# Twelve token runs a batch of 508 and 504 columns in place of ten of 512 and two of 480

## The chip, the cores and the metric

The kernel runs on one core of one Trainium2 chip. The metric is the device time of one execution in microseconds (us). The core has a matrix engine (TensorE, PE in the profile; PEld is its weight load), a vector engine (VectorE, DVE), a scalar engine (ScalarE, ACT), GpSimd (POOL, unused here but for four constants) and a sync engine (SyncE, SP) that issues transfers. Matmul results land in PSUM, which has eight banks of 512 fp32 columns; everything else lies in SBUF.

## What is computed

A gated scan over the tokens of two sequences of 6080 tokens with 256 channels, and then a feed-forward block with 2048 hidden units on all 12160 tokens.

```
f = lower_bound + (1 - lower_bound) * sigmoid(f_logit)
i = 1 - f
for t in range(S):
    h = f[:, t] * h + i[:, t] * x[:, t]
    y[:, t] = h
hid = y.reshape(B * S, D) @ w_in             # 256 -> 2048
g = hid * clip(hid + 3, 0, 6) / 6
out = g @ w_out                              # 2048 -> 256
```

## The kernel before

Everything is kept transposed: channels lie on the 128 partitions, tokens along the columns. The tokens of each of the two sequences are cut into twelve runs, and `token_runs` (L185) lists them in order of position, the two sequences in turn, as (sequence, first token, number of tokens n). With 6080 tokens it makes ten runs of 512 and two of 480 a sequence, 24 runs in all, numbered h = 0 to 23. The n of a run is the number of columns of every matmul, of every ScalarE and VectorE instruction and of every transfer of this run; no other size in the program hangs on it, and all tiles are allocated 512 columns wide whatever n is.

A run goes through these stages:
- `scan_x` (L344) loads f_logit and x, forms the gate on ScalarE and VectorE and runs the scan along the tokens (L387). The last state of a run starts the scan of the next one of the sequence. For h = 0 the work is cut into two halves of n/2 columns.
- `split` (L400) makes two fp32r tensors of each fp32 tensor, the rounded value (hi) and the remainder (lo). A product is then three fp32r matmuls: hi by hi, hi by lo, lo by hi.
- The first product and the gate. The first four runs (`DIRECT`, L109) are `direct` (L569): 16 blocks of 128 hidden units with 6 matmuls each. The other 20 runs go in pairs, one run of each sequence at the same position, through `quad` (L655): a scheme of seven products in place of eight for a block of two by two, 8 quads of 7 products of 3 matmuls a pair (matmuls in `product`, L620). Sums that the scheme needs are taken on ScalarE and VectorE (L599, L609, L611).
- The second product, `mm2` (L499, matmuls in L512), adds up over the hidden blocks in a PSUM bank: 2 halves of 3 matmuls for each block. From the second pair on, the first four blocks (`GROUP`, L21) of the second product go through the seven-product scheme too (`chain`, L738).
- `evict` (L540) scales by 1/6 and stores.

Counted out, the four direct runs have 192 products of 128 x 128 weights each (a few of them are done in fp32 from the unsplit weights, L509 and L585), the first pair has 360 fp32r matmuls and each of the nine later pairs has 354. At the start, fillers on zeros (L836) keep TensorE busy between the first matmuls.

The order on every engine is fixed before the run. Each piece of work is a `Job` with a modelled cost that depends on n (`act_cost`, `dve_cost`, `pe_cost`, L87 to L96); `ordered` (L117) walks through the jobs by due times and gives the order in which each engine's instructions are issued, and this is repeated five times with the starts found. The matmuls of a pair are interleaved with the second product of the pair before it by a fixed table (`FILLS`, L22).

Of the kernel before, what the change touches and what calls it, by code (L numbers as in the profile page):

```python
# [18 lines left out]
BANK = 512  # L19
# [165 lines left out]
def token_runs(B, S):  # L185


    runs = []
    full = (S - 1) // BANK - 1
    rest = S - full * BANK  # L190
    counts = [BANK] * full + [-(-rest // 2), rest // 2]
    assert counts[-1] == counts[-2] <= BANK
    s = 0
    for n in counts:
        runs.extend((b, s, n) for b in range(B))
        s += n
    return runs
# [3 lines left out]
def gated_scan_then_ffn(  # L201
# [10 lines left out]
    NF = w.shape[1]  # L212
    KD = D // P
    runs = token_runs(B, S)
    assert B == 2 and KD == 2 and NF % 4 == 0 and len(runs) > 4 and len(runs) % 2 == 0
    pairs = [(h, h + 1) for h in range(DIRECT, len(runs), 2)]
# [652 lines left out]
```

## Time and profile before

| what | us |
|---|---|
| median of 3 runs (lowest, highest) | 1001.44 (1000.84, 1001.79) |
| the profiled execution, as timed | 1001.43 |
| its span, first to last instruction | 999.6 |
| TensorE busy in it | 988.1 (99%) |
| VectorE busy | 854.0 (85%) |
| ScalarE busy | 691.5 (69%) |

The profiled execution takes 1.83 us more than its span. In the rows further down, an engine's line gives its busy time and its number of instructions. A matmul's recorded time runs until its last result and overlaps the next matmul, so the distance between the starts of two matmuls is shorter than the time of one. The chain of work that ended last is followed back from the last instruction: each piece is work that released the next one or that ran just before it on the same engine, and successive pieces of one line are merged, with their number.

### The profile page before, as it was taken

The numbers are of one execution on the slowest core, as the hardware profiler recorded it, in microseconds if no ns is written. First come the engines' busy times: TensorE is split into PE (matmuls) and PEld (weight loads), VectorE is DVE, ScalarE is ACT, GpSimd is POOL, SyncE is SP. The second block draws the span as 40 slices with busy tenths as digits, with TensorE's granted clock in tenths as the row PEclk, the third lists the DMA queues.
The fourth block names the chain that finished last, engine by engine and source line by source line (L and its number), as shares of the span: only waits on it lengthen the run. The fifth ranks groups of instructions, "written<-read, shape, count | busy, mean of one in ns | idle before, by whom it ended". The sixth has DMA issues, their size and how long they took to land.

```text
span 999.6 us, 11737 instructions
## 1 busy us (share of the span) xinstructions
PE 988.1 (99%) x4343; PEld 811.2 (81%) x4343; DVE 854.0 (85%) x1131; ACT 691.5 (69%) x1101; POOL 0.2 (0%) x4
## 2 busy tenths in 40 slices
PE   9999999999899999999999999999999999999998
PEld 3778888888688888888888888888888888888887
DVE  7997658998999989988988998998998898898863
ACT  7975656666768659668667766866875866866752
POOL 0000000000000000000000000000000000000000
PEclk9999999999999999999999999999999999999999
DMA  9751030010002002003003001100200200300101
GB/s 360 269 168 45 22 106 22 0 64 22 22 32 95 1 22 106 1 3 125 1 0 127 1 1 59 68 0 32 95 1 22 101 1 1 122 0 1 41 1 40
DMA packets 25898, 54.89 MB, mean 55 GB/s; under 512 B 2288, under 2 KB 6896, under 8 KB 25840
## 3 DMA queue, kind: packets, MB, share of 16 engines
q1 hardware_dynamic: 25424, 53.87, 15.1%
q8 instruction: 34, 0.56, 0.2%
q10 hardware_dynamic: 416, 0.26, 0.1%
q14 instruction: 24, 0.20, 0.1%
HBM read 41.67 MB, written 12.45 MB: 54 GB/s over the span
## 4 chain that ended last, share of the span: by engine, by line
PE 94%; DVE 3%; issue 1%; ACT 1%; DMA 0%; SPq 0%; ACTq 0%
PE bank L620 46%; PE bank L512 40%; PE bank L575 8%; PE bank L585 1%; DVE xt L387 1%; DMA wst<-w 0%; DVE xt L377 0%; DVE r L483 0%; PE bank L509 0%; DVE xlo L415 0%; DVE xt L246 0%; ACT ft L365 0%; DVE wst L290 0%; DVE glo L565 0%; ACT xhi L408 0%
## 5 line engine op out<-in xcount | busy, mean ns | idle before, releaser
L481 ACT ACTIVATE r<-bank 128x512 f32<-128x512 f32 (+1 forms) x304 | 179.7, 592 | 136.9 <-PE bank L620 105.9
L483 DVE SCALAR_TENSOR_TENSOR r<-r,bank 128x512 f32<-128x512 f32 (+1 forms) x304 | 205.5, 677 | 47.5 <-ACT r L481 46.4
L512 PE MATMUL bank<-ghi,whi 128*128 128x512 f32 (+1 forms) x620 | 240.5, 388 | 0.0
L512 PE MATMUL bank<-glo,whi 128*128 128x512 f32 (+1 forms) x620 | 240.2, 387 | 0.0
L512 PE MATMUL bank<-ghi,wlo 128*128 128x512 f32 (+1 forms) x620 | 240.2, 387 | 0.0
L620 PE MATMUL bank<-xhi,wst 128*128 128x512 f32 (+1 forms) x640 | 234.6, 387 | 1.7 <-DVE bank L611 1.7
L620 PEld LDWEIGHTS bank<-xhi,wst 128*128 128x128 f32 x640 | 120.1, 188 | 26.0 <-DVE bank L611 2.1
L412 DVE SCALAR_TENSOR_TENSOR glo<-r,ghi 128x1024 fp32r<-128x1024 f32 (+1 forms) x98 | 118.2, 1206 | 23.7 <-ACT ghi L406 23.6
L512 PEld LDWEIGHTS bank<-ghi,wlo 128*128 128x128 f32 x620 | 116.3, 188 | 23.4 <-DVE wlo L294 0.2
L512 PEld LDWEIGHTS bank<-ghi,whi 128*128 128x128 f32 x620 | 116.3, 188 | 23.3 <-issue 0.2
L512 PEld LDWEIGHTS bank<-glo,whi 128*128 128x128 f32 x620 | 116.3, 188 | 23.3
L620 PE MATMUL bank<-xlo,wst 128*128 128x512 f32 (+1 forms) x320 | 123.8, 387 | 0.0
L406 ACT ACTIVATE ghi<-r 128x1024 fp32r<-128x1024 f32 (+1 forms) x98 | 102.6, 1047 | 17.7 <-PE bank L512 9.8
L415 DVE TENSOR_TENSOR glo<-r,ghi 128x1024 fp32r<-128x1024 f32 (+1 forms) x89 | 106.6, 1204 | 3.9 <-ACT ghi L408 3.8
L408 ACT CAST ghi<-r 128x1024 fp32r<-128x1024 f32 (+1 forms) x89 | 92.2, 1037 | 15.2 <-PE bank L512 12.5
L611 DVE TENSOR_TENSOR bank<-bank,e 128x512 f32<-128x512 f32 (+1 forms) x80 | 55.3, 691 | 28.0 <-PE bank L620 20.3
L620 PEld LDWEIGHTS bank<-xlo,wst 128*128 128x128 f32 x320 | 60.0, 188 | 11.9
L481 ACT ACTIVATE r<-e 128x512 f32<-128x512 f32 (+1 forms) x80 | 49.7, 621 | 26.1 <-DVE e L609 26.1
L620 PE MATMUL bank<-xhi,whi 128*128 128x512 f32 (+1 forms) x160 | 62.0, 387 | 1.0 <-ACT bank L599 1.0
L620 PE MATMUL bank<-xlo,whi 128*128 128x512 f32 (+1 forms) x160 | 61.9, 387 | 0.0
L620 PE MATMUL bank<-xhi,wlo 128*128 128x512 f32 (+1 forms) x160 | 61.9, 387 | 0.0
L599 ACT ACTIVATE bank<-bank 128x512 f32<-128x512 f32 (+1 forms) x80 | 46.1, 576 | 22.7 <-PE bank L620 22.3
(95 smaller groups left out, 1369.3 us busy)
## 6 DMA issues: line engine op xcount, KB each, us to landing
outT<-o SPq DMA_DIRECT2D x40, 256.0 KB, 2.0
ft<-fT SPq DMA_DIRECT2D x19, 512.0 KB, 5.1
xt<-xT SPq DMA_DIRECT2D x18, 512.0 KB, 6.0
wst<-w SPq DMA_DIRECT2D x14, 512.0 KB, 4.3
wst<-w SPq DMA_DIRECT2D x14, 511.5 KB, 5.7
ft<-fT SPq DMA_DIRECT2D x4, 480.0 KB, 4.5
xt<-xT SPq DMA_DIRECT2D x4, 480.0 KB, 5.2
outT<-o SPq DMA_DIRECT2D x4, 240.0 KB, 2.0
```

The costliest lines, as they stand in the source:

```text
L387: nc.vector.tensor_tensor_scan(xt.get()[:, k, o:e], ft.get()[:, k, o:e], xt.get()[:, k, o:e], init, op0=ALU.mult, op1=ALU.add if negative ...
L406: nc.scalar.mul(to(hi), cut(src), -1.0)
L408: nc.scalar.copy(to(hi), cut(src))
L412: nc.vector.scalar_tensor_tensor(out=to(lo), in0=cut(src), scalar=-1.0, in1=to(hi).bitcast(F32), op0=ALU.mult, op1=ALU.subtract)
L415: nc.vector.tensor_tensor(to(lo), cut(src), to(hi).bitcast(F32), op=ALU.subtract)
L481: b = job("ACT", act_cost(n, psum=True), lambda: nc.scalar.activation(r.get()[:, i, :n], src.get()[:, :n], AF.Relu, bias=3.0, scale=-1.0 i ...
L483: return job("DVE", dve_cost(n), lambda: nc.vector.scalar_tensor_tensor(out=r.get()[:, i, :n], in0=r.get()[:, i, :n], scalar=6.0, in1=src. ...
L512: nc.tensor.matmul(bank.get()[:, :n], wt[f][:, D + m * P:D + (m + 1) * P], g.get()[:, half, :n], start=(start and i == 0), stop=(stop and ...
L575: nc.tensor.matmul(ph.get()[:, o:e], wt[f][:, k * P:(k + 1) * P], x[h].get()[:, k, o:e], start=(i == 0), stop=(i == len(ops) - 1),)
L599: nc.scalar.mul(out.get()[:, :n], src.get()[:, :n], -1.0)
L611: nc.vector.tensor_tensor(o, x, y, op=ALU.add)
L620: nc.tensor.matmul(bank.get()[:, :n], wt(), x(), start=(start and z == 0 and i == 0), stop=(z == len(parts) - 1 and i == 2), skip_group_ch ...
```

## The change

`token_runs` makes twelve runs a sequence of nearly equal length, in multiples of 4: eight of 508 tokens and then four of 504. Nothing else is edited. The number of runs, pairs, matmuls, other instructions and transfers stays. The direct runs (positions 0 and 1), the first pair (position 2) and the pairs at positions 3 to 7 have 508 columns, those at 8 to 11 have 504. The halves of h = 0 have 254 columns. The first token of a run is now a multiple of 508 up to 4064, and 504 further on from there.

```diff
     runs = []
-    full = (S - 1) // BANK - 1
-    rest = S - full * BANK
-    counts = [BANK] * full + [-(-rest // 2), rest // 2]
-    assert counts[-1] == counts[-2] <= BANK
+    count = -(-S // BANK)
+    base = S // count // 4 * 4
+    longer, rest = divmod(S - count * base, 4)
+    assert not rest and base + 4 * (longer > 0) <= BANK
     s = 0
-    for n in counts:
+    for i in range(count):
+        n = base + 4 * (i < longer)
         runs.extend((b, s, n) for b in range(B))
         s += n
     return runs
```

## Rows read from the trace of the kernel before

**Rows 1.** Busy time and share by engine; chain by engine; span and granted clock
```profile
PE 988.1 (99%) x4343; PEld 811.2 (81%) x4343; DVE 854.0 (85%) x1131; ACT 691.5 (69%) x1101; POOL 0.2 (0%) x4
...
PE 94%; DVE 3%; issue 1%; ACT 1%; DMA 0%; SPq 0%; ACTq 0%
...
core 0: 999.6 us, clock 1.000
```
**Rows 2.** Stretches: length, busy us and instructions by engine, clock, DMA share, GB/s
```profile
0.00:60.00 60.00, 56.81 (x209) 35.82 (x209) 52.10 (x84) 48.70 (x92) 0.20 (x4) 1.00 0.77 280
60.00:200.00 140.00, 139.73 (x616) 115.70 (x617) 106.21 (x163) 86.92 (x149) 0.00 (x0) 1.00 0.16 57
...
264.00:275.00 11.00, 6.49 (x26) 4.41 (x25) 10.93 (x17) 8.10 (x13) 0.00 (x0) 1.00 0.00 0
275.00:825.00 550.00, 550.00 (x2428) 455.40 (x2428) 493.00 (x608) 394.25 (x607) 0.00 (x0) 1.00 0.11 41
...
860.00:999.60 139.60, 136.06 (x628) 117.31 (x627) 105.70 (x139) 85.73 (x135) 0.00 (x0) 1.00 0.08 27
```
**Rows 3.** TensorE's groups, shapes kept apart: count, busy us, mean ns
```profile
L512 PE MATMUL bank<-ghi,whi 128*128 128x512 f32 x524 | 204.3, 390 | 0.0
...
L575 PE MATMUL bank<-xhi,whi 128*128 128x512 f32 x116 | 36.6, 397 | 1.5 <-DVE r L483 1.5
L512 PE MATMUL bank<-ghi,whi 128*128 128x480 f32 x96 | 36.3, 378 | 0.0
...
L620 PEld LDWEIGHTS bank<-xhi,wst 128*128 128x128 f32 x640 | 120.1, 188 | 26.0 <-DVE bank L611 2.1
```
**Rows 4.** The chain in order of time: start us, us, what, matmuls
```profile
31.59 1.39 PE bank L575 x6
...
597.09 1.36 PE bank L512 x6
...
615.45 17.68 PE bank L620 x78
...
837.54 1.39 PE bank L512 x6
...
855.66 16.90 PE bank L620 x78
```
**Rows 5.** TensorE in order of time after a stall and with 480 columns
```profile
273.45 0.39 PE L620 MATMUL bank<-xlo,wst 128*128 128x512 f32 x1
...
274.61 0.39 PE L512 MATMUL bank<-ghi,whi 128*128 128x512 f32 x1
...
899.91 0.38 PE L512 MATMUL bank<-ghi,wlo 128*128 128x480 f32 x1
900.13 0.37 PE L512 MATMUL bank<-glo,whi 128*128 128x480 f32 x1
900.34 0.38 PE L512 MATMUL bank<-ghi,whi 128*128 128x480 f32 x1
```
**Rows 6.** TensorE in order of time: the matmuls that it waited for
```profile
60.27 0.73 PE L575 MATMUL bank<-xhi,whi 128*128 128x512 f32 x2 [1.45 <-DVE r L483]
...
266.44 0.50 PE L620 MATMUL bank<-bhi,whi 128*128 128x512 f32 x1 [1.85 <-DVE e L609]
...
269.08 0.50 PE L620 MATMUL bank<-xhi,whi 128*128 128x512 f32 x1 [0.99 <-ACT bank L599]
...
273.12 0.50 PE L620 MATMUL bank<-xhi,wst 128*128 128x512 f32 x1 [1.68 <-DVE bank L611]
```
**Rows 7.** VectorE in order of time: the same line at two widths
```profile
249.51 1.22 DVE L415 TENSOR_TENSOR glo<-r,ghi 128x1024 fp32r<-128x1024 f32 x1
...
986.50 1.16 DVE L415 TENSOR_TENSOR glo<-r,ghi 128x960 fp32r<-128x960 f32 x1 [1.43 <-ACT ghi L408]
```
**Rows 8.** In order of time: the last matmul and the last eviction
```profile
995.68 0.38 PE L512 MATMUL bank<-glo,whi 128*128 128x480 f32 x1
...
996.10 0.66 DVE L548 TENSOR_SCALAR r<-bank 128x480 f32<-128x480 f32 x1 [3.24 <-PE bank L512]
```

## What the change should do to the time

> **What bounds the kernel now.** I began with the engines' shares and the chain of work that ended last. TensorE is busy for 988.1 of 999.6 us and holds 94% of the chain; the granted clock is 1.000, its level of 2.4 GHz, throughout [rows 1]. The table by stretches says where this is not so: TensorE falls short in the first 60 us, in 264 to 275 us (VectorE 10.93 of 11 us busy) and at the very end. From 275 to 825 us it is never idle, and after that only behind the last matmul [rows 2, 8]. The stalls are the 1.45 us at 60.27 and the three at 266.44, 269.08 and 273.12 of together 4.52 us [rows 6]. So the time is set by the interval from the start of one matmul to the start of the next, and only that can move it by much. A matmul's recorded duration (389 or 378 ns) overlaps its neighbours' and is not the interval.
>
> The intervals come from the chain, whose merged pieces cover a stated number of matmuls without a gap. With 512 columns 78 of them take 17.68 us: 226.67 ns each. With 480, 78 take 16.90 us: 216.67 ns each [rows 4]. At 2.4 GHz a column takes 0.4167 ns, so 512 columns stream in 213.33 ns and 480 in 200.00 ns. What is left beyond streaming is 13.33 ns at 512 and 16.67 ns at 480: the shorter one is dearer by 3.33 ns than the fixed rest would make it. That is the gap on which the change can gain.
>
> The same rows hold a second thing. The interval at 512 is not one number. Six 512-column matmuls at 837.54, right behind matmuls with 480, take 1.39 us, where six normally take 1.36; six early ones among fp32 matmuls take 1.39 too [rows 4]. That is 231.67 ns, 18.33 ns beyond streaming. After the stall at 273.12, the five intervals from 273.45 to 274.61 take 1.16 us, 232 ns each, and from then on the intervals are even again [rows 5]. So 226.67 is a value that 512 settles into after being disturbed, not a plain sum of streaming and a constant. With 480 the settled intervals alternate: the starts from 899.91 on are 0.22 and 0.21 us apart in turn, and two together take 0.43 us, 433.33 ns by the long row [rows 4, 5]. As an estimate from these sums: 226.67 is 34 times 6.667 ns, and 433.33 is 65 times 6.667 ns. Both settled patterns are whole multiples of 6.667 ns, which is 16 columns at 2.4 GHz.
>
> **The change, part by part.** Matmuls. By the groups of matmuls with their shapes kept apart [rows 3], fp32r matmuls with 512 columns are 3 x 524 (second product), 3 x 116 (direct first product) and 1344 + 3 x 98 (L620, in eleven more groups of the same view), together 3558; those with 480 are 3 x 96, 336 and 3 x 28, together 708. The rest of the 4343 are 36 fp32 records and 41 fillers. Run by run these are 720 in the four direct runs, 360 in the first pair and 354 in each of nine later pairs. The change keeps the number, 4266. It gives 508 columns to the direct runs, the first pair and five later pairs (720 + 360 + 5 x 354 = 2850 matmuls) and 504 to four pairs (1416). The columns streamed are 2,161,536 before and 2,161,464 after, so nothing is gained or lost there (0.03 us). Before, the intervals sum to 3558 x 226.67 + 708 x 216.67 = 806.5 + 153.4 = 959.9 us.
>
> No row shows 504 or 508 columns, so their interval is bounded from both sides by the nearest rows. Lower end: 512's settled 13.33 ns beyond streaming holds at any width, that is 225.00 and 223.33 ns; sum 641.2 + 316.2 = 957.5 us, 2.4 us less. Upper end: they never settle and pay 512's unsettled 18.33 ns, that is 230.00 and 228.33 ns; sum 978.8 us, 18.9 us more. Between them: the 480's 16.67 ns gives 228.33 and 226.67 ns, 971.7 us, 11.8 us more. And if a settled interval must be a multiple of 6.667 ns: 33 of them, 220.00 ns, would leave 8.3 or 10.0 ns beyond streaming, less than the 13.33 ns that are the least of any long row, so 34 remain, 226.67 ns for both widths. Then all 4266 take 226.67 ns: 967.0 us, 7.1 us more.
>
> I take the last value. The nearest row is 512's: 508 and 504 lie 4 and 8 columns from it and 28 and 24 from 480. A settled interval is what long rows show, and 225.00 ns can't keep its place in a pattern of 6.667 ns, while 226.67 can. In this reading the columns taken away from the 512s return nothing, and the last 708 matmuls lose the 10.0 ns that their 480 columns had saved: 708 x 10.0 ns = 7.1 us.
>
> The Trainium skill, page "TensorE: Matmul & The Clock Gate", section "Back-to-back issue gap", gives N / 2.4 + 2.5 ns for back-to-back matmuls; by that rule columns and count alone decide, and the change would be worth 0.03 us. The trace disagrees on the constant: the rule gives 215.8 ns for 512 and 202.5 for 480, where the chain shows 226.67 and 216.67 [rows 4].
>
> Weight loads. Their number and shape stay; each takes 188 ns in the groups at every width [rows 3], under the shortest interval, so they add nothing unless 480's interval is a floor that they set, and 504 and 508 lie above that floor.
>
> fp32 matmuls. 36 records lose 4 or 2 columns in two passes: 0.1 us less, before 30 us, where the weights' arrival decides anyway. Taken at 0.
>
> VectorE and ScalarE. Instruction counts stay and columns too. A view of the first n columns of two halves is one run of 1024 now and two runs of 508 later; the 960-column form is already two runs and takes 1.16 us against 1.22 us for 1024 [rows 7], 0.06 us for 64 columns, so the break costs nothing. VectorE is 493 of 550 us busy in the settled stretch [rows 2], 90%, and stays there; in the last pairs it rises from 76% with 504 for 480 columns and stays covered by TensorE. In 264 to 275 us it is the bound; its 10.93 us shrink by at most 4/512, 0.1 us. The order that the planner writes may come out otherwise there: between all 4.52 us saved and as much lost; the row itself says 4.52, and I take no change.
>
> DMA. Loads and stores keep their count; 512 KB become 508 or 504, 480 KB become 504. Rows now start at multiples of 2032 bytes instead of 2048. From 60 us on the queues are busy 0 to 16% [rows 2] and loads are issued ahead, which is the cover; in the first 60 us (77%) four direct runs move 0.8% less. Taken at 0, within 0.2 us.
>
> The end. The last matmul starts at 995.68, the last eviction of 480 columns takes 0.66 us and the span ends at 999.6 [rows 8]. 24 more columns add 0.03 us there by VectorE's 0.06 us for 64 columns, and some hundredths in the transfer: 0.1 us, which meets the 0.1 us saved above.
>
> Sum, against the profiled execution (1001.43 us, 1.83 us above its span, the same as the median of 1001.44): 1001.4 + 7.1 = 1008.5 us.
>
> **The rivals.** Faster: the 13.33 ns hold at any width, and 216.67 ns is a floor that only widths under 488 meet. Place: the last two pairs, 708 x 3.33 ns; the time is 1001.4 - 2.4, and 0.2 us of it goes into the stalls at 60 and 264 us, which don't end earlier because TensorE comes sooner: 999.2 us. It decides if a 508-column matmul takes 225.4 ns or less. For it: 226.67 and 216.67 fit a fixed rest with a floor. Against it: the 231.67 ns rows, which say that the rest is not fixed.
>
> Much slower: 504 and 508 never settle. 971.7 to 978.8 us of intervals, less some tenths hidden in the stalls: 1013 to 1020 us. For it: every stretch that is not settled 512 leaves 16.67 ns or more beyond streaming. Against it: 480 has a settled pattern of its own.
>
> No change: the interval is a straight line through both points, 225.42 and 224.17 ns, sum 959.9 us: 1001.4 us. Only two points speak for it. The rule of the Trainium skill cited above would give this time too.
>
> Half way: 508 keeps 226.67 ns and 504 alternates 33 and 34 times 6.667 ns (223.33 ns): 2.4 us more, 1003.8 us. Or a multiple of 33 for both after all: 21.4 us less; nothing shows so small a rest.
>
> **How the numbers follow.** All short widths at 226.67 ns: 0.36, 1008.5 us. Never settled: 0.25. Fixed rest with floor: 0.18. Straight line: 0.09. Half way: 0.07. 33 multiples: 0.05. The range reaches from the floor's case, 998.8, to the unsettled bound, 1020; that leaves out the last case and the ends of the others. A difference under 0.2% (2.0 us) is about what a measurement of this kernel can't tell from none. Faster than 999.4 takes 0.12 of the floor's 0.18 and the 0.05, and 0.02 for a kinder order at 264 us: 0.19. Within 2.0 us: 0.06 of the floor, 0.08 of the line and 0.01 of the half way: 0.15. Slower: 0.66.
>
> **What would show it.** The chain's merged pieces: 78 matmuls of 508 at 17.68 us and 78 of 504 at 17.68 us bear the forecast; 17.55 and 17.42 us bear the floor; 17.8 us or more the unsettled case. The starts after a stall should be back at even steps within a dozen matmuls. TensorE should stay idle only where it is now; an added stall after 275 us, or the three at 264 us changed by over 1 us, would make the time wrong for another reason than the interval.

## The result and the profile after

The changed kernel takes 1015.15 us (median of 4 runs, 1014.11 to 1015.56); the kernel before took 1001.62 us beside it. The ratio is 1.0134, with a 95% interval of 1.0117 to 1.0152: 13.5 us slower. The forecast was slower by 7.1 us, 1008.5, with a range to 1020. So the sign and the main mechanism came out, and 6.4 us were not in the sum. The profiled execution of the changed kernel took 1014.11 us with a span of 1012.3; against the 1001.43 and 999.6 of before that is 12.7 us, and it is this difference that is taken apart here.

The page of the changed kernel, busy time and instructions by engine, answers to [rows 1]:

```profile
PE 999.6 (99%) x4345; PEld 814.3 (80%) x4346; DVE 855.5 (85%) x1130; ACT 692.8 (68%) x1102; POOL 0.2 (0%) x4
```

So does its span with the mean granted clock:

```profile
core 0: 1012.3 us, clock 0.996
```

Three things differ that the prediction had as unchanged. VectorE has one instruction less (1131 before) and ScalarE one more (1101 before); TensorE has two matmuls more (4343 before), both of them fillers on zeros in the first 60 us, of which there are 43 in place of 41; and the mean clock is 0.996 where it was 1.000. The first is small to look at and turns out to be worth 3 us.

The chain in order of time (start us, us, what, matmuls), as in [rows 4]. The first piece has 508 columns, the others 504:

```profile
540.19 17.75 PE bank L621 x78
...
701.35 17.68 PE bank L621 x78
...
861.83 17.68 PE bank L621 x78
```

With 504, 78 matmuls take the forecast 17.68 us, 226.67 ns each, exactly what 512 took before. With 508 they take 17.75 us, 227.6 ns each: slower than both 504 and 512. (The mean over some 2700 settled intervals with 508 is 227.62 ns.)

The matmuls for which TensorE waited, as in [rows 6]; the number in brackets is the idle time before:

```profile
61.47 0.74 PE L576 MATMUL bank<-xhi,whi 128*128 128x508 f32 x2 [2.87 <-DVE r L484]
...
271.39 0.79 PE L621 MATMUL bank<-xhi,whi 128*128 128x508 f32 x1 [2.52 <-ACT bank L600]
...
277.02 0.50 PE L621 MATMUL bank<-xhi,wst 128*128 128x508 f32 x1 [1.26 <-DVE bank L612]
```

And the table by stretches behind these stalls and in the settled part (length, busy us and instructions by engine, clock, DMA share, GB/s), as in [rows 2]:

```profile
61.40:67.00 5.60, 5.53 (x17) 4.45 (x18) 4.15 (x8) 3.56 (x7) 0.00 (x0) 0.70 0.63 205
271.30:274.60 3.30, 3.21 (x8) 2.62 (x9) 2.90 (x6) 2.61 (x5) 0.00 (x0) 0.54 0.00 0
...
278.00:825.00 547.00, 547.00 (x2407) 451.66 (x2406) 486.23 (x602) 389.13 (x603) 0.00 (x0) 1.00 0.12 41
```

The stall at 60 us has doubled, from 1.45 to 2.87 us, and the granted clock behind it is a mix of its two levels, 0.70 over 5.6 us, where the kernel before had 1.00:

```profile
61.40:67.00 5.60, 5.60 (x26) 4.60 (x25) 5.24 (x10) 4.10 (x7) 0.00 (x0) 1.00 0.82 252
```

At 264 to 278 us the stalls are shorter (2.52 and 1.26 us in place of the three of together 4.52), but there too the clock falls. In the settled part TensorE is never idle, as before.

With the same matmul set beside the same matmul in both traces, the 12.7 us divide like this. Up to 43 us the changed kernel is 0.3 us ahead. From there to 70 us, around the stall, it loses 3.1 us. Then 0.95 ns with each 508-column matmul, about 2.7 us by 700 us. At 264 to 278 us, 0.2 us net. Where 504 stands in place of 512 (700 to 830 us) next to nothing (0.1 us). Where 504 stands in place of 480, 10.0 ns with each of the last 708 matmuls, 7.0 us. The experiments ask three things: what rule gives these intervals, whether the 3.1 us belong to the widths at all, and whether a better choice of widths exists.

### The profile page after: what moved, and what is told of

It reads as the page before. It is cut to its first block, busy times and chain, and to the rows that moved or that the text cites. A ratio compares the mean times of both kernels' runs of the same rounds, so it can differ in the third digit from the quotient of the medians.

```text
span 1012.3 us, 11760 instructions
## 1 busy us (share of the span) xinstructions
PE 999.6 (99%) x4345; PEld 814.3 (80%) x4346; DVE 855.5 (85%) x1130; ACT 692.8 (68%) x1102; POOL 0.2 (0%) x4
## 4 chain that ended last, share of the span: by engine, by line
PE 95%; DVE 2%; ACT 1%; DMA 1%; issue 0%; ACTq 0%; SPq 0%; DVEq 0%
PE bank L621 46%; PE bank L513 41%; PE bank L576 8%; PE bank L586 1%; ACT xhi L409 0%; DMA wst<-w 0%; DVE xt L388 0%; DMA xt<-xT 0%; PE bank L510 0%; DVE xt L378 0%; DVE r L484 0%; DVE xlo L416 0%; ACT r L482 0%; ACT ft L366 0%; ACT ft L375 0%
## 5 line engine op out<-in xcount | busy, mean ns | idle before, releaser
L482 ACT ACTIVATE r<-bank 128x508 f32<-128x508 f32 (+1 forms) x304 | 179.8, 593 | 141.3 <-PE bank L621 108.3
L484 DVE SCALAR_TENSOR_TENSOR r<-r,bank 128x508 f32<-128x508 f32 (+1 forms) x304 | 205.1, 676 | 50.9 <-ACT r L482 49.4
L513 PE MATMUL bank<-ghi,whi 128*128 128x508 f32 (+1 forms) x620 | 241.9, 390 | 0.0
L513 PE MATMUL bank<-ghi,wlo 128*128 128x508 f32 (+1 forms) x620 | 241.2, 389 | 0.0
L513 PE MATMUL bank<-glo,whi 128*128 128x508 f32 (+1 forms) x620 | 241.2, 389 | 0.0
L621 PE MATMUL bank<-xhi,wst 128*128 128x508 f32 (+1 forms) x640 | 235.0, 389 | 1.3 <-DVE bank L612 1.3
L413 DVE SCALAR_TENSOR_TENSOR glo<-r,ghi 128x1016 fp32r<-128x1016 f32 (+1 forms) x98 | 118.2, 1207 | 23.2 <-ACT ghi L407 23.2
L621 PE MATMUL bank<-xlo,wst 128*128 128x508 f32 (+1 forms) x320 | 124.5, 389 | 0.0
L407 ACT ACTIVATE ghi<-r 128x1016 fp32r<-128x1016 f32 (+1 forms) x98 | 102.7, 1048 | 16.8 <-PE bank L513 10.3
L416 DVE TENSOR_TENSOR glo<-r,ghi 128x1016 fp32r<-128x1016 f32 (+1 forms) x89 | 106.6, 1205 | 6.0 <-ACT ghi L409 5.9
L621 PEld LDWEIGHTS bank<-xlo,wst 128*128 128x128 f32 x320 | 60.2, 188 | 12.7
```

Of the source, the lines that this page charges most:

```text
L407: nc.scalar.mul(to(hi), cut(src), -1.0)
L413: nc.vector.scalar_tensor_tensor(out=to(lo), in0=cut(src), scalar=-1.0, in1=to(hi).bitcast(F32), op0=ALU.mult, op1=ALU.subtract)
L416: nc.vector.tensor_tensor(to(lo), cut(src), to(hi).bitcast(F32), op=ALU.subtract)
L482: b = job("ACT", act_cost(n, psum=True), lambda: nc.scalar.activation(r.get()[:, i, :n], src.get()[:, :n], AF.Relu, bias=3.0, scale=-1.0 i ...
L484: return job("DVE", dve_cost(n), lambda: nc.vector.scalar_tensor_tensor(out=r.get()[:, i, :n], in0=r.get()[:, i, :n], scalar=6.0, in1=src. ...
L513: nc.tensor.matmul(bank.get()[:, :n], wt[f][:, D + m * P:D + (m + 1) * P], g.get()[:, half, :n], start=(start and i == 0), stop=(stop and ...
```

## The experiments

**Which interval belongs to which width.** Two kernels carry many widths in one program. Theory A says that settled patterns are made of steps of 6.667 ns; B, streaming and a fixed rest of about 17 ns; C, a straight line between 480 and 512.

```diff
-    full = (S - 1) // BANK - 1
-    rest = S - full * BANK
-    counts = [BANK] * full + [-(-rest // 2), rest // 2]
-    assert counts[-1] == counts[-2] <= BANK
+    counts = [512, 512, 512, 512, 510, 508, 506, 504, 502, 500, 496, 506]
```

> Nine widths in one program: the runs of each batch have 512 (four times), 510, 508, 506, 504, 502, 500, 496 and 506 columns. It is read by the settled interval of each width in TensorE's trace. Theory A, the settled pattern is made of steps of 6.667 ns: 510, 506, 502 and 500 come out like 508 and 504, between 226.67 and 228 ns (500: 226.67), and 496 falls to 33 steps, 220.00 ns. Theory B, streaming and a fixed rest of about 18 ns that 512 alone is spared (as 504's 226.67 could be read, 210.0 + 16.67): 510 229, 506 227.5, 502 225.8, 500 225.0, 496 223.3 ns. Theory C, a straight line between 480 and 512 from which only 508 and 504 stand out: 500 222.9, 496 221.7 ns. The time itself says little: 1008 to 1018 us.

The chain of that run, one piece of second-product matmuls for each width, here in the order 510, 508, 504, 502, 500, 496:

```profile
375.17 17.68 PE bank L617 x78
455.63 17.75 PE bank L617 x78
...
616.74 17.68 PE bank L617 x78
696.97 17.43 PE bank L617 x78
776.43 17.68 PE bank L617 x78
856.16 15.84 PE bank L617 x72
```

The second run has lower widths: `counts = [512, 512, 512, 496, 492, 488, 484, 480, 472, 464, 448, 432]`. It leaves out the last 288 tokens of each sequence, so its time isn't set against the others.

> The runs have 512 (three times), 496, 492, 488, 484, 480, 472, 464, 448 and 432 columns; the last 288 tokens of each sequence are left out, so the time is not to be set against the others. It is read by the settled interval of each width. Theory A (steps of 6.667 ns above a floor): 496 220.00, 492 to 480 between 216.67 and 220, and 472 down to 432 no lower than some floor near 216.67 that weight loads set, since each takes 188 ns and is followed by a matmul. Theory B (streaming and 16.67 ns): 496 223.3, 488 220.0, 480 216.67, 464 210.0, 448 203.3, 432 196.7 ns. A floor without steps: 488 and all below 216.67.

Its chain, in the order 496, 492, 488, 480, 472, 464, 448, 432:

```profile
295.21 17.16 PE bank L617 x78
373.43 17.34 PE bank L617 x78
451.96 17.16 PE bank L617 x78
...
607.55 16.90 PE bank L617 x78
684.13 16.00 PE bank L617 x75
759.38 16.29 PE bank L617 x78
833.07 14.88 PE bank L617 x72
905.32 14.10 PE bank L617 x72
```

The first kernel took 1006.87 us, somewhat under the 1008 to 1018 expected; theory A's own intervals add up to 1006 to 1009 us, so the lower end of that range was set too high. Each piece divided by its count gives the interval. The table has the means over the settled intervals in both traces, where no stall or other width is within eleven matmuls, and what they are in steps of 6.667 ns:

| columns | ns | steps | beyond streaming, ns |
|---|---|---|---|
| 512 | 226.67 | 34 | 13.33 |
| 510 | 226.67 | 34 | 14.17 |
| 508 | 227.6 | 34 1/7 | 15.9 |
| 506 | 226.67 | 34 | 15.83 |
| 504 | 226.67 | 34 | 16.67 |
| 502 | 223.34 | 33 1/2 | 14.17 |
| 500 | 226.67 | 34 | 18.33 |
| 496 | 220.00 | 33 | 13.33 |
| 492 | 222.22 | 33 1/3 | 17.22 |
| 488 | 220.00 | 33 | 16.67 |
| 484 | 218.67 | 32 4/5 | 17.00 |
| 480 | 216.67 | 32 1/2 | 16.67 |
| 472 | 213.33 | 32 | 16.67 |
| 464 | 208.88 | 31 1/3 | 15.55 |
| 448 | 206.66 | 31 | 20.00 |
| 432 | 195.82 | 29 3/8 | 15.82 |

Theory B fails at 496 (223.3 expected, 220.00 found) and at 448, and C fails at 500. The steps hold, but in a weaker form than expected: a settled mean need not be a whole number of steps, it is a whole number over a short cycle. Nine of the sixteen widths have a whole number themselves. With 508 seven intervals repeat (225, 230, 232, 233, 224, 227, 222 ns in this trace's rounding) and take 239 steps. In these two kernels only 512 and 496 reach the least rest, 13.33 ns. And there is no floor at 216.67 ns, so that part of theory A fails: 432 columns take 195.8. With this the rival of a fixed rest above a floor is dead in both its parts.

**Whether the 3 us come from the widths.** The changed widths with every instruction of every engine in the order of the kernel before: the planner runs first with the old runs, and its order is used. (A list in the source that names the column 256, the subject of the next experiment, gets 254 beside it.)

```diff
+    if not plan:
+        return [(jobs.index(j), j.start, j.end) for j in order]
+    order = []
+    for i, start, end in plan:
...
+        order.append(jobs[i])
```

> The widths of the change, 508 and 504, but every instruction in the order of the kernel before on every engine, with the second half-run of the first run scaled on VectorE as before. Theory O, the 3 us at 58 to 70 us come from the planner's other order (and from the scaling that the change moves from VectorE to ScalarE by its column number): the stall at 60 us is back to 1.5 us, no clock fall behind it, 1011.5 to 1012.5 us. Theory W, they come from the widths themselves: stall and clock fall stay, 1015 us. The intervals, 227.6 ns at 508 and 226.67 at 504, stay in both.

It took 1010.83 us (1010.56 to 1011.53), 1.0094 of the kernel before with an interval of 1.0079 to 1.0109, 4.3 us less than the changed kernel and a little under the 1011.5 to 1012.5 expected. TensorE's stall at 60 us:

```profile
60.47 0.72 PE L613 MATMUL bank<-xhi,whi 128*128 128x508 f32 x2 [1.51 <-DVE r L521]
```

The stretch behind it:

```profile
61.40:67.00 5.60, 5.60 (x27) 4.60 (x26) 5.25 (x10) 4.05 (x7) 0.00 (x0) 1.00 0.79 227
```

Stall and clock are those of the kernel before, and matmul for matmul its span of 1009.3 us exceeds the 999.6 by 2.6 us in the 508s and 7.0 us in the last 708. Theory O holds: the widths cost 9.6 us, and the rest is a matter of order. In the profiled executions that rest is 3.0 us (1012.3 against 1009.3), less than the 4.3 between the medians; the profiled execution of the changed kernel is the fastest of its four, and what the others lose beyond it wasn't traced.

**Where the other order comes from.** The kernel has a list of the scalings that VectorE takes over from ScalarE, and it names them by run and first column:

```
SHARED = ((0, 0), (0, 256), (1, 0))
...
                    if k and (h, o) in SHARED:
```

The first run is worked on in two halves. With 512 columns the second one starts at 256; with 508 it starts at 254 and is no longer in the list. So the change, which touches `token_runs` alone, moves one scaling of 254 columns from VectorE to ScalarE. That is the instruction by which the counts differ. One run of the changed widths has the list mended, the planner being free:

```diff
-SHARED = ((0, 0), (0, 256), (1, 0))
+SHARED = ((0, 0), (0, 254), (1, 0))
```

> The change with one number mended: the list of pieces whose scaling VectorE takes names the second half of the first run as (0, 254) instead of (0, 256), so that this scaling is back on VectorE; the planner orders the rest itself. Theory S, the moved scaling alone starts what was lost at 58 to 70 us: the stall at 60 us is back to 1.5 us, no clock fall behind it, 1011 to 1012 us. Theory P, the planner's new costs for 508 columns would have reordered ScalarE and VectorE anyhow: the stall stays near 2.9 us and the time near 1015 us.

1010.98 us (1009.88 to 1011.84), ratio 1.0094 (1.0080 to 1.0108); in the profiled execution TensorE's stall at 59.52 us is 1.12 us and the clock is 1.00 throughout. The planner's other costs for 508 columns, which still give an order of their own, are worth nothing that these runs show. The opposite experiment moves the scaling alone, in the kernel before with its 512 and 480 columns:

```diff
-SHARED = ((0, 0), (0, 256), (1, 0))
+SHARED = ((0, 0), (1, 0))
```

> The kernel before, widths 512 and 480, with one entry of the list of shared scalings taken out, so that ScalarE scales the second half of the first run, as it does after the change. If that step alone costs what the change lost at 58 to 70 us, the stall at 60 us is near 2.9 us with a clock fall behind it and the time 1004.3 to 1005.6 us. If it does so only together with the widths, 1001.3 us.

1004.66 us (1004.31 to 1005.53), ratio 1.0034 (1.0021 to 1.0048): 3.4 us by the medians and 3.2 us by the spans (1002.8 against 999.6), without any change of width. How one scaling of about 0.6 us becomes 3 us is to be read from the chain of waits. First the kernel before, then this one:

```profile
50.74 4.62 DMA wst<-w
...
56.14 0.08 ACT last L394
56.22 0.95 ACT xhi L408
...
58.34 0.68 DVE wst L290
59.02 0.60 DVE wst L287
59.62 0.60 DVE r L483
60.23 0.04 issue
60.27 3.04 PE bank L575 x12
```

```profile
51.46 4.61 DMA wst<-w
...
56.84 0.08 ACT last L394
56.92 0.64 ACT wst L285
57.56 0.95 ACT xhi L408
...
59.76 0.60 DVE wlo L294
60.36 0.60 DVE wst L287
60.96 0.61 DVE r L483
61.57 0.04 issue
61.61 2.58 PE bank L575 x8
```

In the order that the planner writes with one more step on ScalarE early on, the loading of a weight stage starts 0.72 us later, and ScalarE has a step of the weights (`wst` at L285, 0.64 us) ahead of the `xhi` on which TensorE's next matmul hangs through `xlo` and the queue of VectorE. (How the planner comes from the one step to this order wasn't followed.) Together 1.36 us; the matmul comes at 61.61 in place of 60.27, 1.34 us later. The rest is the clock. The stall in this kernel, in order of time, and then the stretch behind it:

```profile
61.61 0.73 PE L575 MATMUL bank<-xhi,whi 128*128 128x512 f32 x2 [2.56 <-DVE r L483]
```

```profile
61.40:67.00 5.60, 5.39 (x17) 4.28 (x18) 4.29 (x8) 3.45 (x7) 0.00 (x0) 0.70 0.62 194
```

Behind the idle 2.56 us the granted clock is 0.70 over 5.6 us, a mix of 1.2 and 2.4 GHz. At 0.70 of full speed, 5.6 us hold 3.9 us of work: 1.7 us more. The sum, 1.36 + 1.7 = 3.1 us, meets the 2.9 us that the same matmuls show at 90 us. The changed kernel's stall of 2.87 us with its 0.70 is the same event.

**A better choice of widths.** If 512 and 496 are the only widths with the least rest, eight runs of 512 and four of 496 should beat both kernels.

```diff
-    counts = [BANK] * full + [-(-rest // 2), rest // 2]
+    counts = [512] * 8 + [496] * 4
```

> Eight runs a batch of 512 and four of 496 columns in place of ten of 512 and two of 480: 2850 matmuls with 512 and 1416 with 496. Theory A: 496 takes 220.00 ns, the sum is 646.0 + 311.5 = 957.5 us against 959.9 before, so 999.0 us, 2.4 us faster. Theory C (221.67 ns): 959.9, no change, 1001.4. Theory B (223.3): 962.2, 1003.8 us. If 496 stays at 226.67 like 504: 967.0, 1008.5 us. In each case the planner's order may move the stalls at 60 and 264 us by up to 3 us.

999.33 us (998.59 to 999.72), ratio 0.9977 (0.9969 to 0.9986): 2.0 us faster than the kernel before, where theory A said 2.4. Its chain, with 496 columns:

```profile
695.75 17.16 PE bank L617 x78
```

220.0 ns each, as foretold. The missing 0.4 us could be the planner's order, so the same widths were also put into the order of the kernel before.

> Widths 512 (eight) and 496 (four) a batch with every instruction in the order of the kernel before. If the 0.4 us by which 512 and 496 missed the sum of their intervals come from the planner's order at 264 us (the clock was at 0.77 in 264 to 271 us there), this is 999.0 us or 0.3 to 0.5 us below the other; if not, both take the same.

999.10 us (998.54 to 999.59), ratio 0.9976 (0.9965 to 0.9986): no difference that these runs can tell. Its stretch from 264 us:

```profile
264.00:271.30 7.30, 5.05 (x16) 3.26 (x15) 7.02 (x12) 4.39 (x8) 0.00 (x0) 0.77 0.00 0
```

Up to the first 496-column matmul near 700 us this program has the same instructions in the same order as the kernel before, whose clock was 1.00 in the profiled execution [rows 2]. Here it is 0.77, and 0.5 us are lost. So the order is not what lowers the clock at that place. What does is open; the stall just ahead of it is 1.85 us in both. The mean clock differs between executions of one program, too, and that accounts for the missing 0.4 us: of the eleven executions of the first run with these widths, the five with a mean clock of 1.000 took 998.59 to 998.99 us and the six with 0.997 or 0.998 took 999.33 to 999.72. Beside them, the nine executions of the kernel before with 1.000 took 1001.07 to 1001.37. Median against median at 1.000 the gain is 2.4 us, as theory A said. (Where the clock fell is known for the profiled executions alone.)

**The interval by itself.** Bursts of 36 matmuls at the end of the kernel before, when the other engines have no work left:

```diff
+        for n, o, m in BURSTS:
+            for i in range(36):
+                nc.tensor.matmul(out[:m, :n], whi[i % 4][:, :m], whi[5 + i % 4][:, o:o + n], start=True, stop=True)
```

> The kernel before with bursts of 36 fp32r matmuls at its end, one width each (512 to 384, some from column 4 or 8 of the moving operand, some with 64 weight columns), with no other engine at work, and three bursts of bf16. If the interval belongs to the matmul and its weight load alone, each burst settles at the interval that the width had inside the kernel (512 226.67, 508 227.6, 504 226.67, 496 220.00, 492 222.2, 488 220.0, 480 216.67, 448 206.67, 432 195.8 ns), and a start at column 4 or 8 changes nothing. If neighbours (other engines' reads and writes, or the changing buffers) bring it, the bursts come out on one line, streaming and a constant. If the weight load sets the rest beyond streaming, 64 weight columns shorten it. 1001.4 us and some 200 us for the bursts.

It took 1187.39 us. From starts in the trace, the last two dozen intervals of each burst: 512, 510, 506 and 504 settle at 226.67 ns, 508 in the same cycle of seven, 492 at 222.2, 488 at 220.0, 480 at 216.67, 432 at 195.8, and 384 at 173.33 (26 steps). So neither the other engines nor the kernel's buffers make the steps. Three widths differ from the kernel: 500 gives 223.33 (226.67 there), 496 gives 223.33 (220.00 there), 448 gives 202.7 (206.67 there). Starting at column 4 or 8 of the moving operand leaves 488 at 220.0 (from column 8) and 504 at 226.67 (from 4); 496 shows 223.3 from column 4, with steps of 218 and 228 in turn, and 224.4 from column 8. With 64 weight columns 512 takes 230.0 ns, longer than with 128, and 508 takes 224.4, shorter (12.8 ns beyond streaming); 480 stays at 216.67. So a narrower weight changes the pattern, and not in one direction. The bf16 bursts behind them (512, 508, 480, all on zeros and with one weight tile) are one piece of the chain:

```profile
1162.01 22.79 PE bank L847 x108
```

That is 211.0 ns on average, and their intervals are 215.83, 214.17 and 202.50: streaming and 2.5 ns at each width. All settled intervals of a burst are alike within 1 ns, where those of 508 in fp32r run from 222 to 234. (The means alone wouldn't tell: over a cycle of eight, 215.83 ns too is a whole number of steps.) The last experiment asks what picks the pattern of 496. In each burst of the second series six short bf16 matmuls come first, and in some then twelve of 512:

```diff
+            for i in range(lead):
+                nc.tensor.matmul(outs[0], whi[i % 4][:, :P], whi[5 + i % 4], start=True, stop=True)
+            for i in range(36):
+                out = outs[i // 3 % 3 if rotate else 0]
```

> Bursts of 36 fp32r matmuls again, one after the other with six short bf16 matmuls between: 496 columns into one PSUM bank (223.33 ns in the first burst run), into three banks in turn, and both behind twelve matmuls of 512; 500, 448, 504, 508 and 480 into three banks; 512 and 496 with one and the same weights; 512 and 496 with 32 weight columns. Theory H, a width has more than one settled interval and what came before picks one: 496 behind 512 takes 220.00 ns, from a cold start 223.33; 500 comes out at 223.33 or 226.67. Theory K, the banks pick it: 496 into three banks 220.00 with and without 512 ahead, into one bank 223.33 in both. If neither, the traffic of the other engines does, and all stay at 223.33. 504 226.67, 508 227.6 and 480 216.67 in each case.

TensorE in order of time; the bursts of 496 into three banks without and into one and three banks with 512 ahead:

```profile
1004.52 8.29 PE L849 MATMUL bank<-whi,whi 128*128 128x496 f32 x36
...
1012.84 2.99 PE L846 MATMUL bank<-whi,whi 128*128 128x512 f32 x12
1015.66 8.08 PE L849 MATMUL bank<-whi,whi 128*128 128x496 f32 x36
...
1023.77 3.01 PE L846 MATMUL bank<-whi,whi 128*128 128x512 f32 x12
1026.62 8.08 PE L849 MATMUL bank<-whi,whi 128*128 128x496 f32 x36
```

Behind 512 the intervals of 496 are 220.0 ns from the first one on, whatever the banks; without, they run between 220 and 227 in a cycle with a mean of 223.3. Theory H holds for 496 with 128 weight columns: a width can have more than one settled pattern, and what came before picks it. With 32 weight columns 496 settles at 220.0 without any 512 of full width ahead, so the weight matters too. For 500 it does not show: 223.3 with and without, and what gave 226.67 in the kernel is open. 448 came out at 206.67 here and at 202.7 in the first bursts. 504, 508 and 480 were 226.67, 227.62 and 216.7 again, and 512 with 32 weight columns took 231.8. With one and the same weights in every matmul, 512 (226.7) and 496 (223.3) came out as with four.

## Why the prediction was right in its direction and short in its size

**What bounds the kernel.** Right: the interval from one matmul to the next sets the time, and 9.6 of the 12.7 us are intervals (the run in the old order).

**504 at 34 steps of 6.667 ns.** Right to the digit: 226.67 ns, nothing gained in place of 512, 10.0 ns lost in place of 480, 708 times, 7.0 us where 7.1 stood in the sum.

**508 at 34 steps.** The step was mis-sized. The prediction took 226.67 ns, 15.0 beyond streaming; it measured 227.6, in a cycle of seven that takes 239 steps. 2850 times 0.95 ns is 2.7 us. The working spoke of whole multiples, though it had a half one before it in the 480s' 65 steps over two; a mean over a longer cycle was the open door, and the "never settles" rival (230.0 for 508) was not it either, since the cycle repeats exactly.

**"VectorE and ScalarE. Instruction counts stay."** This step failed, and it is the one a reader could have caught. It counted by the diff and not by what reads the changed numbers; the description of the kernel before, by which no other size hangs on the n of a run, has the same mistake. The new starts of the half runs, 254 for 256, were in the description of the change; the list that compares with 256 was in the source. The cost is 3.1 us: 1.4 us of stall at 60 us and 1.7 us at the lower clock behind it. The prediction gave the stall at 60 us some 0.2 us, and had no term for the clock.

**The order at 264 us.** Taken at no change, with 4.5 us either way. Net 0.2 us: shorter stalls, 3.78 in place of 4.52 us, and a clock of 0.54 over 3.3 us behind the first. The value held, but by two effects against each other.

**Taken at nothing: DMA, the end, the fp32 matmuls, VectorE's split views.** In the run with the old order, all but some 0.2 us of the 9.6 is accounted for by matmul intervals, so these terms are as small as they stood. That they are zero singly wasn't tried.

**The rivals.** The floor at 216.67 ns is shown false by 432 columns at 195.8, the fixed rest by 504 in the change itself, the straight line by 500 and 504. The "33 multiples" case holds for 496 and not for 508 or 504. The "never settle" case foretold 1013 to 1020 us, and the measured 1015.15 lies there, but by chance: 504 settles at 226.67 and 508 in its cycle, and 3.1 us of the time have nothing to do with intervals. That the range reached far enough is owed to this rival, not to the step that failed.

Added up: 7.0 us (504 for 480), 2.6 (508) and 3.1 (the moved scaling) are 12.7, the whole difference of the profiled executions. The 0.8 us by which the medians differ more are not traced.

## What to carry to other kernels

Before the columns of a TensorE-bound fp32r kernel are made even, measure the interval of each candidate width in the kernel itself: here 512 and 496 cost 13.33 ns beyond streaming and their neighbours up to 18.33, so the uneven split was the faster one, and 8 x 512 + 4 x 496 was faster still by 2 us. When a size changes, search the source for every constant that equals the old size or a fraction of it, and compare instruction counts by engine: a list entry of 256 that no longer matched cost 3 us here. A longer stall has to be priced with the clock behind it: at 60 us a wait longer by 1.4 us cost 3.1.

## What the runs showed of the hardware

**The steps belong to fp32r.** Settled fp32r intervals are whole numbers of 6.667 ns over cycles of one to eight matmuls at each of the sixteen widths of the sweeps; bf16 matmuls go by streaming and 2.5 ns. The weight loads differ with the type: one of 128 x 128 takes 188 ns in fp32r and 98 ns in bf16. The Trainium skill, page "TensorE: Matmul & The Clock Gate", section "Back-to-back issue gap", gives that line, N / 2.4 + 2.5 ns, as the gap of an isolated matmul, and about 131 ns at 512 columns for a stream of weight loads and matmuls. For the bf16 bursts, which are such a stream, the trace agrees with the line (215.83 ns at 512), for fp32r it doesn't (226.67), and no run here shows 131. What makes the steps is open: narrower weights change the pattern (512 takes 226.67, 230.0 and 231.8 ns with 128, 64 and 32 weight columns; 496 behind no 512 takes 223.3 with 128 and 220.0 with 32), but a narrower weight changes the load (188, 134 and 108 ns) and the number of result rows together, and no run here parts the two. The bf16 bursts were on zeros; whether the values matter wasn't tried.

**Patterns have a memory.** 496 columns take 220.0 ns behind 512 and 223.3 behind six short bf16 matmuls, in one program and with the same operands. In the kernels 496 took 220.0 behind 512 and, in the first sweep, among and behind 500 at 226.67; in the first burst run, behind 500 at 223.33, it took 223.33. With eight runs of 512 and four of 496 it kept its 220.0 for 1344 settled intervals.

**The clock behind stalls.** Idle 2.56 and 2.87 us at 60 us were followed by a clock of 0.70 over 5.6 us; idle 1.12 to 1.94 us at the same place, in eight kernels, by 1.00. But at 264 us the same instructions behind the same stall of 1.85 us gave 1.00 in the kernel before and 0.77 with 8 x 512 and 4 x 496 in its order; and the first burst run, which is the kernel before up to 996 us, shows 0.69 over 264 to 275 us. So the length of a stall alone doesn't decide.
